# Attention and spectral mixing on one core: q and k transposed together, the opening sums in another order, idle products early

## The chip, the cores and the metric

The kernel runs on one core of a Trainium2 chip. The metric is the device time of one execution in microseconds (us). The time before is the median of three runs. The profile is one further execution, recorded by the hardware profiler.

The engines are called as in the profile: PE is TensorE's matrix product, PEld its weight load, DVE is VectorE, ACT is ScalarE, POOL is GpSimd and SP is SyncE. In this kernel POOL issues the loads from memory, SP issues the stores and the small copies.

## The reference

There are 8 batches and 8 heads, 576 tokens, 64 channels a head. The first part is causal attention with a bias that grows with the distance, the second part a mixing over the first 64 frequencies of the token axis, with a complex 512 x 512 weight for each frequency.

```python
scores = scale * np.matmul(q, k.transpose(0, 1, 3, 2))
cum = np.cumsum(np.maximum(s, 0.0), axis=-1)
bias = -(cum[:, :, :, None] - cum[:, :, None, :])
scores = np.where(causal, -1e9, scores + np.minimum(bias, 0.0))
attn = softmax(scores)
x = np.matmul(attn, v)                         # heads side by side: (8, 576, 512)

X = np.fft.rfft(x, axis=1)                     # Xr, Xi: its first 64 modes
Yr = einsum('bmd,mde->bme', Xr, w_r) - einsum('bmd,mde->bme', Xi, w_i)
Yi = einsum('bmd,mde->bme', Xr, w_i) + einsum('bmd,mde->bme', Xi, w_r)
u = x + np.fft.irfft(Yr + 1j * Yi, n=576, axis=1)
out = u + np.maximum(u @ w_ch, 0.0)
```

The two mode weights, `w_r` and `w_i`, are 64 x 512 x 512 numbers each.

## The kernel before, in words

**Order.** The order of the work on every engine is the order in which the program writes it. Nothing is moved by a planner. Each engine works through its own list, and an instruction that must wait holds back all that follows it on the same engine.

**Attention.** A step `n` (0 to 31) is one batch and one pair of heads: `g = n // 8` is the group of 128 channels, `b = n % 8` the batch. The loop at L564 writes for each step, in this order: the loads for step `n + 3` and some blocks of mode weights; `scores(n, 0)`; `av(n - 1, 1)`; the products of the mode blocks that are due; `transposes(n + 1, 0)`; `scores(n, 1)`; in the last six steps `first_transposed`; `transposes(n + 1, 1)`; `fft(n - 1)`; `av(n, 0)`; and in the last six steps `first_product`, `first_transposed`, `first_product`.

**The transposes.** q and k of a step lie together in one tile `qk2`: partitions 0 to 63 hold q of two heads, 64 to 127 hold k, and each partition holds a run of 18 tokens of one head. `transposes(n, half)` (L332) turns 9 of the 18 tokens of each run. For each it makes one product for q and one for k, 64 x 64 each (L340), into the partition halves of one tile `tr_ps`; that tile has one buffer (L557). Then two copies of 576 elements a partition (L344) take the result to `qt` and `kt`. For half 0 both are on DVE; for half 1 q is on DVE and k on ACT.

**Mode weights.** They come in 128 blocks of 512 KB, four for each of the 8 chunks `c` of 8 modes and each of the 4 groups `g`, two transfers a block. All are issued by POOL (L234), in order, between the loads of q, k and v, into a ring of tiles. `modes(g, c)` (L455) makes 16 products from the four blocks of a chunk: `x` = 0 and 1 use `w_r`, `x` = 2 and 3 use `w_i`. Results of the groups 0 to 2 are added up in `y_acc`; group 3 follows after attention.

**After attention.** The loop at L833 goes over the chunks 0 to 5 of group 3. After a chunk's products DVE makes `yb`, PE transposes it (`y_transposed`), ACT copies it out, and from chunk 4 on PE multiplies it by `w_ch` (`y_times_wch`). `work()` fills in between with products of x and `w_ch` for output pairs that end later. `gather` reorders the rows of several chunks for the inverse transform. A pair is two tiles of 128 tokens; pairs 0 and 1 are finished first. For each, `x_transposed(i)` (L629) transposes x by 8 or 16 products and two DVE copies, and `x_times_wch(i, False)` (L644) makes 8 products of 512 columns. Pair 0's stand in chunk 5, pair 1's stand in chunk 6, at L853 and L855, between the products of chunk 6 and its `y_times_wch`.

**Chunk 7.** L868 calls `modes` with work in between: before `x` = 2 it does `first_u` (pair 0's sum u: x, the rows of chunks 0 to 5, chunk 6) and `first_z(0)`, before `x` = 3 it does `first_z(1)`. `first_z` needs `vb6`, which is chunk 6's product with `w_ch`; `first_u` doesn't. After `x` = 3 come chunk 7's own `yb`, its transpose, its product, and then a written list of steps (L924) that finishes the 18 pairs.

Of the kernel before, what the change touches and what calls it, by code (L numbers as in the profile page):

```python
# [9 lines left out]
FP32 = mybir.dt.float32  # L10
FP16 = mybir.dt.float16
BF16 = mybir.dt.bfloat16
# [6 lines left out]
def kernel(  # L19
# [11 lines left out]
    nc = tc.nc  # L31
    B, H, S, D = q.shape
    NM = moe_w_r.shape[0]
    DM = H * D
    P = 128
# [4 lines left out]
    NG = DM // P  # L40
# [6 lines left out]
    NCK = NM // MC  # L47
# [4 lines left out]
    RP = P // 4  # L52
    R = S // RP
    RH = R // 2
    W = 2 * P
    NWN = S // W
    NK = 2 * NWN
    HM = NM // 2
    HP = P // 2
# [3 lines left out]
    negm_np = np.concatenate(  # L63
        [np.where(2 * np.arange(P)[:, None] + r > np.arange(W)[None, :], -1.0e9, 0.0) for r in range(2)],
        axis=1,
# [55 lines left out]
    NQ = 2  # L121
    qt = [ap_.tile([P, 2, S], BF16, name=f"qt{i}") for i in range(NQ)]
    kt = [ap_.tile([P, 2, S], BF16, name=f"kt{i}") for i in range(NQ)]
# [3 lines left out]

    v2 = [ap_.tile([P, 2 * NWN * W + P], FP16, name=f"v2_{i}") for i in range(NV)]

# [3 lines left out]
    for w in range(NWN):  # L133
        for r in range(2):
            poff.append(poff[-1] + SP - w * W)
    p_sb = [ap_.tile([P, poff[-1]], FP16, name=f"p_sb{i}") for i in range(NP_)]
    p4 = [ap_.tile([P, P], FP16, name=f"p4_{i}") for i in range(2)]

    temp = xs_flat[1].bitcast(FP32)
    ident32, negm32, s_sb = temp[:, :P], temp[:, P : P + 2 * W + NL], temp[:NPAIR, -S:]  # L140
    ident16 = ap_.tile([P, P], BF16, name="ident16")
# [4 lines left out]
    loaded = {}  # L146
# [98 lines left out]
    for n in range(N):  # L245
# [3 lines left out]
        while nt < min(w, len(wq)):  # L249
            i = ring_of(nt)  # L250
# [36 lines left out]
    with tc.tile_pool(name="cum_psum", bufs=1, space=PSUM) as cpsum:  # L287
        spos = s_sb
        zer, cum = (p_sb[i][:NPAIR, :].bitcast(FP32)[:, :S] for i in (0, 1))
        nc.vector.memset(zer, 0.0)  # L290
        nc.vector.tensor_scalar(out=spos, in0=s_sb, scalar1=0.0, scalar2=None, op0=ALU.max)
        nc.vector.tensor_tensor_scan(
            out=cum, data0=spos, data1=zer, initial=0.0, op0=ALU.add, op1=ALU.add
        )
        nc.vector.tensor_scalar(out=ncum_sb, in0=cum, scalar1=-8.0, scalar2=None, op0=ALU.mult)
        ct_ps = cpsum.tile([P, NK + 1, NPAIR], FP32, name="ct_ps")
        keys = cum[:, : NF * P].rearrange("c (w p r) -> c w r p", p=P, r=2)
        for x in range(NK):
            nc.tensor.transpose(
                ct_ps[:, x, :], keys[:, x // 2, x % 2, :], ident32[:NPAIR, :NPAIR]  # L300
            )

        tl = p_sb[2][:NPAIR, :].bitcast(FP32)[:, : 2 * NL].rearrange("p (x t) -> p x t", x=2)
        for x in range(2):
            nc.vector.tensor_copy(out=tl[:, x, :], in_=cum[:, (NT - 1) * P :])
        nc.tensor.transpose(
            ct_ps[:, NK, :], tl.rearrange("p x t -> p (x t)"), ident32[:NPAIR, :NPAIR]
        )
        nc.vector.tensor_copy(out=cumt_sb, in_=ct_ps)
        for x in range(2):  # L310
            rows = slice(NL * x, NL * x + NL)
            nc.vector.tensor_copy(
                out=cumt4[rows, :], in_=cumt_sb[rows, NK, x::2]
            )
# [17 lines left out]
    def transposes(n, half):  # L332
        if n >= N:
            return
        src = loaded[n][:, n % 2, :].rearrange("p (r d) -> p r d", d=D)[:, half * RH : half * RH + RH]
        ps = trpool.tile([P, RH, 2 * RP], BF16, name="tr_ps", tag="tr")
        for r in range(RH):
            for i in range(2):
                rows = slice(HP * i, HP * i + HP)
                nc.tensor.transpose(ps[rows, r, :], src[rows, r, :], ident16[rows, rows])  # L340
        for i, dst in enumerate((qt, kt)):
            copy = (nc.vector.tensor_copy, nc.scalar.copy)[half * i]
            to = dst[n % NQ][:D].rearrange("d h (p r) -> d h p r", r=R)
            copy(  # L344
                out=to[:, :, :, half * RH : half * RH + RH],
                in_=ps[HP * i : HP * i + HP].rearrange("d r (h p) -> d h p r", h=2),
            )

    def scores4(n, ps):

# [205 lines left out]
    with tc.tile_pool(name="sc_psum", bufs=2, space=PSUM) as scpool, \  # L556
# [7 lines left out]
        for n in range(N):  # L564
# [11 lines left out]
            i = first_pairs[n - N + len(first_pairs)] if n >= N - len(first_pairs) else None  # L576
# [52 lines left out]
    def x_transposed(i):  # L629
        xts[i] = xt_sb[len(xts) % 2]  # L630
        for x, (b, T) in enumerate(pairs[i]):
            ps = upool.tile([P, DT, P], FP32, name="xt_ps", tag="u")
            for rows, bb, ident in parts(b, T):
                for dt in range(DT):
                    nc.tensor.matmul(
                        ps[:, dt, rows], x_all[: rows.stop - rows.start, dt, bb, T, :],
                        ident, start=True, stop=True, skip_group_check=True,
                    )
            nc.vector.tensor_copy(out=xts[i][:, x], in_=ps)  # L639

    def start_z(i, x):
        zs[i, x] = zpool.tile([P, DM], FP32, name="z_ps", tag=f"z{i % 2}{x}")

    def x_times_wch(i, last):  # L644
        for x in range(2):
            start_z(i, x)
            for dt in range(DT):
                nc.tensor.matmul(  # L648
                    zs[i, x], xts[i][:, x, dt, :], wch_sb[:, dt, :],
                    start=(dt == 0), stop=(last and dt == DT - 1), skip_group_check=True,  # L650
                )
# [25 lines left out]
    def y_times_wch(c, yt):  # L677
        vp = auxpool.tile([P, DM], FP32, name="v_ps", tag="aux")
        for dt in range(DT):
            nc.tensor.matmul(  # L680
                vp, yt[:, dt, :], wch_sb[:, dt, :], start=(dt == 0), stop=(dt == DT - 1)
            )
        vb = spool.tile([P, DM], FP16, name="v_sb", tag="v")
        nc.vector.tensor_copy(out=vb, in_=vp)
        spread(c, 1, vb)
        return vb

    def gather(c0, c1, turns, kinds):

        n = 2 * MC * (c1 - c0)  # L690
        rows = slice(2 * MC * c0, 2 * MC * c1)
        ng = P // n
        for b0 in range(0, B, ng):
            for which in kinds:
                ps = auxpool.tile([P, DM], FP32, name="g_ps", tag="aux")
                for dt in range(DT):
                    for g in range(ng):
                        op = yt_first[:, dt, : c1 - c0].rearrange("p c (x b) -> p (c x) b", b=B)
                        nc.tensor.matmul(
                            ps[n * g : n * g + n, :] if which else ps[n * g : n * g + n, bass.ts(dt, P)],  # L700
                            op[:, :, b0 + g],
                            wch_sb[:, dt, :] if which else ident16h,
                            start=(dt == 0 or not which), stop=(dt == DT - 1 or not which),
                            tile_position=(0, n * g), skip_group_check=True,
                        )
                for g in range(ng):
                    dst, src = yv[rows, b0 + g, which, :], ps[n * g : n * g + n, :]
                    if g % 2:
                        nc.vector.tensor_copy(out=dst, in_=src)
                    else:  # L710
                        nc.scalar.copy(out=dst, in_=src)
            if b0 // ng in turns:
                work()
# [119 lines left out]
    for c in range(NCK - 2):  # L833
        yb = modes(NG - 1, c)
        for x in range(TAKE[c] - 1):
            work()
        if c == NCK - 3:
            x_transposed(0)
        yt = y_transposed(yb, c)
        if TAKE[c]:  # L840
            work()
        if c >= NY:
            if c == NCK - 3:
                x_times_wch(0, False)
            y_times_wch(c, yt)
            if c == NCK - 3:
                gather(NY, NCK - 2, (), (0,))
        elif c == NY - 1:
            gather(0, NY, (1, 3), (1, 0))
    assert not order_z and not ahead  # L850
    c = NCK - 2
    yb6 = modes(NG - 1, c)
    x_transposed(1)  # L853
    yt = y_transposed(yb6)
    x_times_wch(1, False)  # L855
    vb6 = y_times_wch(c, yt)


    def first_u():
        add_x(0)  # L860
        add_y(u_of(0), 0, 0, slice(0, GK))
        add_last(u_of(0), 0, yb6, c=0)

    def first_z(i):
        add_y(z_of(i), i, 1, slice(0, GK))
        add_last(z_of(i), i, vb6, c=0)

    yb = modes(NG - 1, NCK - 1, {2: lambda: (first_u(), first_z(0)), 3: lambda: first_z(1)})  # L868

    yt = spool.tile([P, DT, P], FP16, name="yt_sb", tag="yt")  # L870
    for x in range(2):
        dts = slice(x * DT // 2, (x + 1) * DT // 2)
        ps = auxpool.tile([P, DT // 2, P], FP16, name="yt_ps", tag="aux")
# [49 lines left out]
    for step in (  # L923
# [8 lines left out]
        i = int(step[1:].rstrip("ab"))  # L932
# [34 lines left out]
```

The softmax here doesn't subtract the row's maximum and nothing guards it: scores larger than these inputs give would overflow.

## Time and profile before

| | |
|---|---|
| time before, median of three runs | 443.91 us (443.87 to 444.06) |
| span of the profiled execution | 442.4 us |
| mean granted TensorE clock | 0.916 |
| PE busy | 340.4 us, 77% |
| DVE busy | 253.3 us, 57% |
| ACT busy | 226.2 us, 51% |
| POOL busy, most of it issuing loads | 246.1 us, 56% |
| moved by DMA | 93.25 MB, mean 211 GB/s |

A busy share is an average over stages with different limits. The stages are: attention to 336 us, the chunks 0 to 6 of group 3 from 336 to 403 us, chunk 7 to 411 us, and the finishing of the pairs to the end. The chain of waits follows the work back from the last instruction, each time to what released it. A granted clock of 0.50 means that products take twice as long as at 1.00.

### The profile page before, as it was taken

The page shows a single profiled execution, that of the slowest core. Times are in us where ns is not written, and L with a number is a line of the kernel's source. Part 1 is how long each engine was busy: PE and PEld are TensorE (multiplying, and loading weights), DVE is VectorE, ACT ScalarE, POOL GpSimd, SP SyncE. Part 2 cuts the span into 40 slices and gives each one's busy share as a digit, 9 for nine tenths or more (in the row PEclk, how much of TensorE's full clock was granted, in tenths as well). Part 3 has the DMA queues.
Part 4 walks back from the last instruction along what each step waited for, and adds up shares of the span by engine and source line. Part 5 has one row for each costly group of instructions (what it writes and reads, how often), then busy time and mean ns, then how long its engine had stood idle before and what let it go on. Part 6 is the DMA issues. An engine that isn't in the chain of part 4 may idle for free.

```text
span 442.4 us, 10783 instructions
## 1 busy us (share of the span) xinstructions
PE 340.4 (77%) x4364; PEld 208.2 (47%) x4411; DVE 253.3 (57%) x574; ACT 226.2 (51%) x421; POOL 246.1 (56%) x385
## 2 busy tenths in 40 slices
PE   1788988988776996593946918888887987759994
PEld 0455665655444653361634505555653445423441
DVE  7766776665645664462633605767655454442696
ACT  1476787365645643472543604665660534320794
POOL 7766565565565656455655546455544444440495
PEclk9998999998969798987895978999997999988998
DMA  9999999999999999999999999999999999997498
GB/s 180 202 208 204 204 206 205 206 207 206 208 195 206 205 208 205 209 206 209 203 206 206 208 207 198 207 206 206 202 209 211 209 209 210 210 217 150 147 388 344
DMA packets 72768, 93.25 MB, mean 211 GB/s; under 512 B 29760, under 2 KB 31296, under 8 KB 72720
## 3 DMA queue, kind: packets, MB, share of 16 engines
q0 software_dynamic: 63408, 81.29, 104.9%
q1 hardware_dynamic: 9312, 11.29, 7.6%
q8 instruction: 34, 0.56, 0.5%
q14 instruction: 14, 0.11, 0.1%
HBM read 163.51 MB, written 9.44 MB: 391 GB/s over the span
## 4 chain that ended last, share of the span: by engine, by line
DMA 60%; PE 19%; DVE 7%; POOL 6%; issue 4%; ACT 2%; POOLq 0%; DVEq 0%
DMA w_sb<-in_moe_w_i_dram 31%; DMA w_sb<-in_moe_w_r_dram 16%; DMA qk<-in_k_dram 8%; PE yp L463 4%; PE sc_ps L382 3%; DMA x_all<-in_moe_w_r_dram 2%; POOL w_sb L234 2%; DMA qk<-in_q_dram 2%; PE sc_ps L376 2%; DMA y_acc<-in_moe_w_r_dram 2%; PE z_ps L546 2%; DVE xt L538 2%; DVE xs L453 1%; PE z_ps L648 1%; PE av_ps L418 1%
## 5 line engine op out<-in xcount | busy, mean ns | idle before, releaser
L390 ACT ACTIVATE p_sb<-sc_ps,cumt_sb 128x576 f16<-128x576 f32 (+1 forms) x256 | 141.7, 635 | 34.3 <-PE sc_ps L382 33.9
L234 POOL DMA_DIRECT2D w_sb<-in_moe_w_r_dram x120 | 71.2, 595 | 63.2 <-DMA w_sb<-in_moe_w_i_dram 16.7
L234 POOL DMA_DIRECT2D w_sb<-in_moe_w_i_dram x120 | 70.9, 593 | 53.0 <-DMA w_sb<-in_moe_w_i_dram 18.7
L344 DVE COPY qt<-tr_ps 64x576 bf16<-64x576 bf16 x64 | 47.8, 747 | 55.7 <-PE tr_ps L340 55.6
L234 POOL DMA_DIRECT2D v<-in_v_dram x72 | 52.0, 722 | 36.6 <-DMA w_sb<-in_moe_w_r_dram 7.6
L382 PE MATMUL sc_ps<-qt,kt 128*128 128x320 bf16 (+2 forms) x337 | 66.7, 303 | 7.2 <-ACT kt L344 3.4
L340 PE MATMUL tr_ps<-ident,qk 64*64 64x64 bf16 x1152 | 35.4, 206 | 38.9 <-DMA qk<-in_k_dram 18.0
L463 PE MATMUL yp<-w_sb,xs 128*32 128x512 bf16 (+1 forms) x480 | 43.2, 413 | 23.8 <-DMA w_sb<-in_moe_w_i_dram 16.8
L361 ACT ACTIVATE p<-sc_ps,cumt 128x64 f16<-128x64 f32 x32 | 10.0, 313 | 88.7 <-PE sc_ps L357 88.7
L376 PE MATMUL sc_ps<-negm,ident 128*128 128x256 bf16 x256 | 53.8, 295 | 0.0
L382 PEld LDWEIGHTS <-kt 128*128 128x128 bf16 x384 | 39.0, 105 | 31.1 <-ACT kt L344 8.8
L340 PEld LDWEIGHTS <-qk 64*64 64x64 bf16 x1152 | 26.9, 119 | 55.2 <-DMA qk<-in_k_dram 19.0
L418 PE MATMUL av_ps<-v,p_sb 128*128 128x65 f16 x1024 | 43.8, 197 | 1.4 <-DVE x_all L428 1.0
L418 PEld LDWEIGHTS <-p_sb 128*128 128x128 f16 x1024 | 37.4, 99 | 8.5 <-DVE x_all L428 3.7
L453 DVE CAST xs<-ft_ps 64x128 bf16<-64x128 f32 x128 | 36.6, 286 | 3.7 <-PE ft_ps L443 2.2
L463 PEld LDWEIGHTS <-xs 128*32 128x32 bf16 (+1 forms) x512 | 19.3, 144 | 41.3 <-DMA w_sb<-in_moe_w_i_dram 15.0
L423 DVE TENSOR_REDUCE den<-av_ps 128x5 f32<-128x10 f32 x64 | 10.8, 169 | 41.4 <-PE av_ps L418 40.4
L428 DVE TENSOR_TENSOR x_all<-av_ps,rcp 128x320 f16<-128x320 f32 x64 | 31.5, 492 | 2.2
L344 ACT COPY kt<-tr_ps 64x576 bf16<-64x576 bf16 x32 | 22.9, 715 | 15.4 <-DVE qt L344 14.8
L443 PE MATMUL ft_ps<-Ff_sb,x_all 128*64 128x192 f16 (+1 forms) x320 | 25.2, 274 | 1.0 <-DVE x_all L428 1.0
L648 PE MATMUL z_ps<-wch_sb,xs 128*128 128x512 f16 x96 | 25.3, 412 | 0.2 <-DVE xs L639 0.2
L344 DVE COPY kt<-tr_ps 64x576 bf16<-64x576 bf16 x32 | 24.4, 762 | 0.4
(113 smaller groups left out, 423.9 us busy)
## 6 DMA issues: line engine op xcount, KB each, us to landing
w_sb<-in_moe_w_r_dram POOLq DMA_DIRECT2D x120, 256.0 KB, 8.4
w_sb<-in_moe_w_i_dram POOLq DMA_DIRECT2D x117, 256.0 KB, 9.0
out_dram<-r_w SPq DMA_DIRECT2D x16, 512.0 KB, 2.8
v<-in_v_dram POOLq DMA_DIRECT2D x72, 64.0 KB, 7.4
qk<-in_q_dram POOLq DMA_DIRECT2D x15, 288.0 KB, 8.3
qk<-in_k_dram POOLq DMA_DIRECT2D x15, 288.0 KB, 9.2
x_all<-in_moe_w_i_dram POOLq DMA_DIRECT2D x6, 256.0 KB, 8.0
y_acc<-in_moe_w_r_dram POOLq DMA_DIRECT2D x4, 256.0 KB, 7.0
```

What stands on the lines that cost most here:

```text
L234: nc.gpsimd.dma_start(out=dst, in_=src)
L340: nc.tensor.transpose(ps[rows, r, :], src[rows, r, :], ident16[rows, rows])
L344: copy(out=to[:, :, :, half * RH : half * RH + RH], in_=ps[HP * i : HP * i + HP].rearrange("d r (h p) -> d h p r", h=2),)
L376: nc.tensor.matmul(ps[:, bass.ds(w * S, W)], ident16, negm[:, bass.ts(r, W)], start=True, stop=False, skip_group_check=True,)
L382: nc.tensor.matmul(ps[:, c0 : c0 + i1 - i0], keys[:, w, r, :], qh[:, i0:i1], start=False, stop=True, skip_group_check=True,)
L390: nc.scalar.activation(out=pt[:, poff[x] : poff[x] + S - w * W], in_=ps[:, w * S : (w + 1) * S - w * W], func=ACTF.Exp, bias=cumt_sb[:, x, ...
L418: nc.tensor.matmul(ps[:, I, r : r + NCH], lhsT, rhs, start=(i == 0), stop=(i == len(todo) - 1), skip_group_check=True,)
L428: nc.vector.tensor_tensor(out=x_all[:, g, b, :, D * h : D * h + D], in0=ps[:, :, 1 : NCH], in1=rcp.unsqueeze(2).to_broadcast([P, NT, D]), ...
L443: nc.tensor.matmul(ps[HP * q_ : HP * q_ + HP].rearrange("p h f -> p (h f)"), x_all[:nT, g, b, T, q_::2], Ff_sb[:nT, T, :], start=(T == 0), ...
L453: nc.vector.tensor_copy(out=xs[g % 2][HP * h : HP * h + HP, q_, :, h, :, b, :], in_=a)
L463: nc.tensor.matmul(ps[32 * cg : 32 * cg + 32, :], cols[k0:, q_, 1 - ri, :, c * MC // 2 + cg], wt[(g, c, ri, cg // 2)][k0:, 2 * (cg % 2) + ...
L648: nc.tensor.matmul(zs[i, x], xts[i][:, x, dt, :], wch_sb[:, dt, :], start=(dt == 0), stop=(last and dt == DT - 1), skip_group_check=True,)
```

## The change

It has three parts.

1. **q and k transposed together.** A product now takes 64 channels of all 128 partitions, q and k at once: its result has 64 partitions, with 64 columns of q and 64 of k side by side. Tokens 0 to 8 of each run go to the first half of the result's partitions (`y` = 0), tokens 9 to 17 to the second (`y` = 1). Half 0 does token indices 0 to 4 of both, 10 products; half 1 indices 5 to 8, 8 products. The copies are now by token half and by q or k: four of 320 elements for half 0, four of 256 for half 1. The aim is fewer products.
2. **Idle products early.** 50 products of the identity with 64 of its own columns, whose result nobody reads, stand on PE ahead of the first transposes of the cumulative sums. The aim is a TensorE that has left its slow clock when attention starts.
3. **Opening sums re-ordered.** Pair 1's `x_transposed` and `x_times_wch` go from chunk 6 into chunk 5; and in chunk 7 both `first_z` stand before `x` = 2, `first_u` before `x` = 3. The aim is less work on PE behind the last weights.

```diff
+    SPLIT = (0, (RH + 1) // 2, RH)
...
+        idle_ps = cpsum.tile([P, HP], FP32, name="idle_ps")
+        for i in range(50):
+            nc.tensor.matmul(idle_ps, ident16, ident16[:, :HP], start=True, stop=True, skip_group_check=True)
...
-        src = loaded[n][:, n % 2, :].rearrange("p (r d) -> p r d", d=D)[:, half * RH : half * RH + RH]
-        ps = trpool.tile([P, RH, 2 * RP], BF16, name="tr_ps", tag="tr")
-        for r in range(RH):
-            for i in range(2):
-                rows = slice(HP * i, HP * i + HP)
-                nc.tensor.transpose(ps[rows, r, :], src[rows, r, :], ident16[rows, rows])
-        for i, dst in enumerate((qt, kt)):
-            copy = (nc.vector.tensor_copy, nc.scalar.copy)[half * i]
-            to = dst[n % NQ][:D].rearrange("d h (p r) -> d h p r", r=R)
-            copy(
-                out=to[:, :, :, half * RH : half * RH + RH],
-                in_=ps[HP * i : HP * i + HP].rearrange("d r (h p) -> d h p r", h=2),
-            )
+        r0, r1 = SPLIT[half : half + 2]
+        src = loaded[n][:, n % 2, :].rearrange("p (y r d) -> p y r d", y=2, d=D)
+        ps = trpool.tile([P, SPLIT[1], P], BF16, name="tr_ps", tag="tr")
+        for r in range(r0, r1):
+            for y in range(2):
+                nc.tensor.transpose(ps[HP * y : HP * y + HP, r - r0, :], src[:, y, r, :], ident16)
+        for y in range(2):
+            for i, dst in enumerate((qt, kt)):
+                copy = nc.scalar.copy if half and i else nc.vector.tensor_copy
+                to = dst[n % NQ][:D].rearrange("d h (p y r) -> d h p y r", r=RH, y=2)
+                copy(
+                    out=to[:, :, :, y, r0:r1],
+                    in_=ps[HP * y : HP * y + HP, : r1 - r0, HP * i : HP * i + HP].rearrange(
+                        "d r (h p) -> d h p r", h=2
+                    ),
+                )
...
             if c == NCK - 3:
                 x_times_wch(0, False)
+                x_transposed(1)
             y_times_wch(c, yt)
             if c == NCK - 3:
                 gather(NY, NCK - 2, (), (0,))
+                x_times_wch(1, False)
...
-    x_transposed(1)
     yt = y_transposed(yb6)
-    x_times_wch(1, False)
     vb6 = y_times_wch(c, yt)
...
-    yb = modes(NG - 1, NCK - 1, {2: lambda: (first_u(), first_z(0)), 3: lambda: first_z(1)})
+    yb = modes(NG - 1, NCK - 1, {2: lambda: (first_z(0), first_z(1)), 3: first_u})
```

## The prediction

> **What bounds the kernel now.** I read the strip of 40 slices first, then the queues, then the chain in order of time, and last the single transfers and windows around 400 us.
>
> ```profile
> DMA  9999999999999999999999999999999999997498
> q0 software_dynamic: 63408, 81.29, 104.9%
> ```
>
> For 36 of 40 slices, to 398 us, the DMA engines are over 90% busy, and the queue of loads that POOL fills asks for more than the whole span of 16 engines. So attention and the chunks 0 to 6 run beside a stream of loads that has no gap to give. Windows of 2 us between 20 and 396 us hold 184 to 225 GB/s, nearly all 195 to 213. The chain in order of time says what happens when the stream nears its end:
>
> ```profile
> 386.01 10.89 DMA w_sb<-in_moe_w_i_dram
> 396.91 0.04 issue
> 396.95 1.07 PE yp L463 x4
> 398.02 0.96 PE xt_ps L635 x16
> 398.98 0.54 PE yt_ps L672 x4
> 399.52 3.18 PE z_ps L648 x8
> 402.70 0.86 PE v_ps L680 x4
> 403.56 0.59 PE yp L463 x8
> ...
> 406.43 0.58 PE yp L463 x4
> ...
> 408.00 0.60 PE yp L463 x4
> ```
>
> From 396.95 to 408.6 PE is never idle, so 4.14 us of pair 1's work (0.96 + 3.18) look like a straight saving. They aren't, because eight more transfers were issued after the one that landed at 396.9. The last of them in the timeline, and the answer for its tile:
>
> ```profile
> 397.19 0.59 POOL L234 DMA_DIRECT2D w_sb<-in_moe_w_i_dram  x1 [0.70 <-DMA w_sb<-in_moe_w_i_dram]
> ```
> ```profile
> DMA to landing us min/median/max: 10.2/10.2/10.2
> ```
>
> It lands at 397.19 + 10.2 = 407.4. The same reading of the other seven gives 398.2, 399.5, 400.8, 402.0 for chunk 7's `w_r` and 403.3, 405.4, 406.2 for the first three of its `w_i`. The four products of `x` = 3 need the last one, and they start at 408.0. PE is thus only 0.6 us behind the stream. That 0.6 us is what part 3 can earn while the stream stays where it is.
>
> The windows of the clock:
>
> ```profile
> 392.30:395.70 3.40, 1.09 (x10) 0.48 (x10) 2.08 (x4) 1.73 (x3) 1.42 (x3) 0.96 1.10 208
> 395.70:399.10 3.40, 2.15 (x24) 1.26 (x25) 1.05 (x3) 0.00 (x0) 1.18 (x2) 0.50 1.13 220
> 399.10:402.50 3.40, 3.40 (x12) 1.29 (x11) 0.85 (x2) 0.58 (x1) 0.00 (x0) 0.54 1.12 210
> ```
>
> PE was busy a third of the first window and then ran at half clock (third number from the right) to 402.3. That is why eight products of 512 columns took 3.18 us there, against 1.90 us for the same eight at 387.8.
>
> **What the Trainium skill says.** "TensorE: Matmul & The Clock Gate", Part 1: the clock is halved after an idle window of about 3.4 us and restored after a busy one, and the windows run freely. The trace agrees: restored at 344.2 and 402.3, which is 17 times 3.41 us apart; half busy (336 us) was not enough to keep it, a full window restored it. "PSUM — Partial Sum Buffer", Terms: two engines on one bank and quadrant at once collide, so their accesses must be kept apart. In this trace they are kept apart by tile, even where the partitions differ: ACT's first k copy waited for DVE's q copy of the other half, though its input was long ready.
>
> ```profile
> 14.05 0.75 DVE L344 COPY qt<-tr_ps 64x576 bf16<-64x576 bf16 x1 [0.79 <-PE tr_ps L340]
> ```
> ```profile
> 14.83 0.71 ACT L344 COPY kt<-tr_ps 64x576 bf16<-64x576 bf16 x1 [12.58 <-DVE qt L344]
> ```
>
> "DMA: Bandwidth & Descriptors", Queues, rings and completion order: an engine takes turns between queues. So a small copy from SP takes its share at once and delays the weights; no run yet shows how much.
>
> **Part 1, the transposes.** A step had 36 products; now 18. Before, 18 took 0.47 us; with 0.206 for one, that is (0.47 - 0.206) / 17 = 16 ns each. The new ones have twice the columns. Products into two partition halves do run side by side here (four of L755, 512 columns, took 0.43 us, two at full width also 0.43), so a pair of 128 columns costs about a quarter of 214 ns: 10 products 5 x 53 + 206 = 0.47 us, 8 products 0.42. PE gains nothing to speak of; without the overlap it would lose 0.4 us a step.
>
> The copies cost more. DVE's 128x256 and 128x512 copies from `v_ps` take 424 and 692 ns: 156 + 1.047 ns an element, which gives 759 for 576 where the rows show 747 to 762. So 320 elements take 491 and 256 take 424 ns. Half 0: 4 x 491 = 1.96 us for 0.747 + 0.762 = 1.51, plus 0.45. Half 1 on DVE: 0.85 for 0.75, plus 0.10. ACT: its 256- and 512-element copies take 372 and 589, so two of 256 take 0.75 to 0.9 for 0.715. DVE in all: 32 x 0.55 = 18 us more.
>
> There is a new wait. The four copies of half 1 read one tile in the order DVE, ACT, DVE, ACT, so DVE's second must wait for ACT's first, and that stands behind the four exponentials of `scores(n, 1)`. In the step at 285 us these end at 289.03 and DVE would be at its second copy at 289.0; it gets it at 289.55 instead. Behind it on DVE wait the four `xs` casts, the division of `av` and the cast `xt` (done at 291.53), for which PE waited 0.99 us before `first_product`. I get 0.45 + 0.10 + 0.55, about 1.1 to 1.2 us a step on that path; 0.55 if the copies of different halves need not wait, 1.7 if ACT's copies are slower.
>
> In the steps up to 25 PE waits for q and k (30 us in all) and for weights (17 us), which hides it. In the last six, from 276 us, PE waits for no load; five of them have transposes, so attention ends some 6 us later (3 to 8.5). Who notices? Weight block k of the last groups takes the tile of block k - 11. I put the issue times beside the products' times: the tightest are block 107, issued 5.6 us after its tile came free, and block 123, 3.2 us. A later issue must moreover first eat the 10 us of transfers that are queued. PE itself has waits of 1.9 us at 355.7 and about 0.7 at 385 to give back, and 2 us at 395. So some 3 us may be left at chunk 5; the stream does not stop.
>
> **Part 2, the idle products.** At half clock a column takes 427 / 512 = 0.83 ns, so 50 of 64 columns take 2.7 us. Their input is there at 6.57, and the next PE work waited to 9.73 for the scan on DVE. Hidden; if each also paid for its own weight load, 107 ns, they would end at 11.9 and attention would start 2 us later, into waits for q and k. Cost at the end: 0 both ways.
>
> **Part 3.** Pair 1's two parts go into chunk 5. `x_transposed(1)` takes 0.64 us there (as at 360.7) and two DVE copies of 0.65 ahead of `v_sb`; the gather and chunk 6's `yp` tile move by 0.7. `x_times_wch(1)` takes 1.9 and fills PE's wait of 1.88 us for DVE before 393.7. Chunk 6 then still waits for 396.9. From there: 0.65 products, 0.75 `y_sb`, 0.4 to 0.6 transpose, 0.65 ACT, 0.9 to 1.75 `v_ps`, 0.75 `v_sb`: `vb6` at 401.2 to 402.2. `x` = 1 waits for 402.0. Both `first_z`, 0.86 + 0.98 warm, to 404.2, or 3.5 cold, to 405.9. `x` = 2 waits for 405.4. `first_u` is six products of 0.214, 1.3 us. PE is at `x` = 3 at 407.1 warm, about 407.5 if the clock comes back at 405.7 (two windows after 398.9). So the stream decides: 407.4. But `v_sb`'s 128 KB, sent at 404.3 before, now go out at 402, in full traffic. The hardware queue's 7.6% of 442.4 us for 11.29 MB is 3.0 us a MB, so up to 0.4 us. I take 0.25: `x` = 3 at 407.7 instead of 408.0. What follows is unchanged. Sum: 443.9 - 0.3 = 443.6.
>
> **The rivals.**
> A, the saving comes through: the stream itself gets earlier, or the tail loses more than its last wait. For: PE is gapless to 408.6. Against: the landing at 407.4. The full 4.1 us would give 439.8; a stream 0.5 us earlier and the 0.6 give 442.8, the likely form.
> B, the clock: PE is idle more between 397 and 405, stays at half clock to as late as 408.8, and `first_u` takes 2.6. Then `x` = 3 starts at 408.9: 444.9. For: 1.1 us busy of the 3.4 before 399. Against: both `first_z` keep PE busy from 402.4.
> C, attention's copies: the lag is 8 us or more, chunk 6 starts at 400 or later and blocks come late: x = 3 at 409.5, 445.4. For: DVE is the chain in the last steps. Against: the tiles' slack.
>
> **How the numbers follow.** Stream decides, 443.6: 0.62. A 0.17, B 0.12, C 0.09. The range takes in A's likely form and B and the near side of C: 442.7 to 445.2. Faster by 0.2% is below 443.0: A, 0.18. Slower is above 444.8: B and C, 0.20. Within: 0.62.
>
> **What would show it.** The last weight lands at 407.2 to 407.9 and `x` = 3 follows within 0.2 us. `tr_ps` copies: 490 and 424 ns, DVE some 18 us busier, a wait of DVE for ACT `kt`. Attention ends at 339 to 345 instead of 336. The DMA strip stays at 9 to slice 36. I am wrong if the last landing moves by over 1 us, or if `x` = 3 starts well after it.

## The result and the profile after

The changed kernel takes 450.51 us (median of six runs, 448.81 to 451.57). The kernel before takes 444.17 us beside it (443.87 to 445.12). The ratio is 1.0136, 95% interval 1.0112 to 1.0159: slower by 6.3 us. The prediction was 443.6 us with a range from 442.7 to 445.2.

In the changed kernel's line numbers everything below the transposes stands 7 lines lower than before: the products `yp` are L470 instead of L463, the loads are L235 instead of L234. These are lines of the profile page after: busy time, the strip of 40 slices, the queue of loads, the shares of the chain by engine, and two groups of copies (busy us, mean ns, then the idle time before them and its releaser).

```profile
PE 339.7 (76%) x3847; PEld 200.9 (45%) x3885; DVE 274.2 (61%) x670; ACT 232.5 (52%) x453; POOL 246.3 (55%) x385
DMA  9999999999999999999999999999999999994398
q0 software_dynamic: 63408, 81.29, 103.7%
PE 33%; DVE 27%; DMA 24%; ACT 9%; issue 4%; POOL 2%; SPq 0%; POOLq 0%; DVEq 0%; ACTq 0%
L349 DVE COPY qt<-tr_ps 64x256 bf16<-64x256 bf16 (+1 forms) x128 | 65.3, 510 | 50.6 <-PE tr_ps L344 29.0
L349 ACT COPY kt<-tr_ps 64x256 bf16<-64x256 bf16 x64 | 30.4, 475 | 31.4 <-DVE qt L349 29.9
```

PE has not gained (340.4 us before). DVE is busy 20.9 us more, ACT 6.3 us more. The strip still reads 9 to slice 36, so by the strip alone nothing has changed. The chain has: before, DMA held 60% of it, PE 19% and DVE 7%. Now PE and DVE hold 60% together, and the loads 24%.

The chain in order of time, near the end of the loads (start, us, what):

```profile
387.96 1.83 PE z_ps L655 x8
389.79 1.07 PE yp L470 x14
390.89 0.70 DVE y_sb L494
...
393.81 1.05 PE yp L470 x11
394.88 0.57 DVE y_sb L494
...
404.83 0.70 DVE y_sb L494
406.01 0.59 ACT yt_sb L681
406.65 1.04 PE v_ps L687 x4
407.69 0.99 PE yp L470 x8
...
413.82 0.60 PE yp L470 x4
```

Before, this chain ran through the landing of a weight block at 396.9. Here no load stands in it from 380 us on. The four products of `x` = 3 start at 413.8 instead of 408.0, and the 5.8 us between are nearly the whole loss: the program ends 33.9 us after the last `y_sb` addition (DVE's first work on chunk 7's products) starts in this kernel, 33.7 us in the one before.

PE's waits between 336 and 412 us say the same (us in total, times, longest). Before, one line of its answer was

```profile
PE yp L463 <- DMA w_sb<-in_moe_w_i_dram: 4.2, 3, 2.1
```

After, the answer has no line with a load in it. It begins

```profile
PE yt_ps L679 <- DVE y_sb L494: 3.6, 4, 1.7
PE g_ps L706 <- DVE yv L716: 2.0, 2, 1.0
PE ft_ps L450 <- DVE x_all L435: 1.0, 1, 1.0
```

The last weight block lands at 408.6 us, 1.2 us later than before, and `x` = 3 starts some 5 us behind it; before, it was 0.6 us. Both are signs that the prediction had named for being wrong. So the end is no longer set by the loads but by the work after attention, and that starts later. The last two divisions of the attention on DVE, before and then after:

```profile
330.99 0.49 DVE L428 TENSOR_TENSOR x_all<-av_ps,rcp 128x320 f16<-128x320 f32 x1
334.26 0.49 DVE L428 TENSOR_TENSOR x_all<-av_ps,rcp 128x320 f16<-128x320 f32 x1
```
```profile
342.12 0.49 DVE L435 TENSOR_TENSOR x_all<-av_ps,rcp 128x320 f16<-128x320 f32 x1
345.39 0.49 DVE L435 TENSOR_TENSOR x_all<-av_ps,rcp 128x320 f16<-128x320 f32 x1
```

The last one is 11.1 us late. I call this the lag. Of it 5.3 us are absorbed (I call this the slack) and 5.8 us remain. The stretch from this division to the last `y_sb` shows where the 5.3 us come from. Before, PE is busy 60.4 of its 74.4 us; after, 58.7 of 69.0 us. So 3.7 us are idle time of PE that is gone, the waits for weights above all. The other 1.6 us are busy time: PE runs at half clock for 10.2 us of the stretch after and for 13.7 us before, one window of the clock less.

One step's copies in the timeline of the kernel after (DVE and ACT only; in brackets the idle time before and its releaser):

```profile
276.39 0.50 DVE L349 COPY qt<-tr_ps 64x320 bf16<-64x320 bf16 x1
276.80 0.49 DVE L349 COPY kt<-tr_ps 64x320 bf16<-64x320 bf16 x1
277.31 0.55 DVE L349 COPY qt<-tr_ps 64x320 bf16<-64x320 bf16 x1
277.75 0.52 DVE L349 COPY kt<-tr_ps 64x320 bf16<-64x320 bf16 x1
...
278.91 0.57 DVE L349 COPY qt<-tr_ps 64x256 bf16<-64x256 bf16 x1
279.52 0.57 ACT L349 COPY kt<-tr_ps 64x256 bf16<-64x256 bf16 x1
280.13 0.43 DVE L349 COPY qt<-tr_ps 64x256 bf16<-64x256 bf16 x1 [0.64 <-ACT kt L349]
...
280.58 0.37 ACT L349 COPY kt<-tr_ps 64x256 bf16<-64x256 bf16 x1 [0.49 <-DVE qt L349]
```

The 0.64 us ahead of DVE's last copy is the new wait that the prediction had named. DVE has it in each of the five steps with transposes after 276 us, 3.2 us together.

The lag does not grow evenly, though. These are the starts of `x_all` of head 0 by step, late against before, in us (worked out from the timelines):

```text
step                        26    27    28    29    30    31
after                      1.1   2.5   5.4   8.1   9.4  11.1
```

Two steps cost 1.3 to 1.4 us. Three cost 1.7 to 2.9. What differs there is in the windows of the clock (PE busy us first, granted clock third from the right):

```profile
287.94:291.36 3.42, 2.83 (x46) 1.88 (x44) 2.70 (x7) 2.69 (x6) 2.39 (x5) 1.00 1.21 203
291.36:294.77 3.41, 1.39 (x10) 0.54 (x9) 2.55 (x8) 0.91 (x2) 2.08 (x4) 1.00 1.24 206
294.77:298.18 3.41, 3.19 (x27) 2.21 (x26) 0.00 (x0) 2.44 (x5) 1.87 (x4) 0.55 1.15 209
```

PE stood behind the delayed `xs` and `xt` of DVE (0.87 and 1.15 us), was busy 1.39 of 3.41 us, and then ran at half clock for a window. It happened three times, at 295.1, 308.8 and 332.7 us. These times are 4 and 7 times 3.41 us apart, so the windows go on in even steps; in the three windows just ahead of them PE was busy 41% each time. No sharp bound shows: in the same trace windows of 56% and 59% (from 281.5 and 319.0 us) kept the clock and one of 71% (from 346.3 us) lost it. Before, the clock stood at 1.00 from 270 to 336 us.

### The profile page after: what moved, and what is told of

It reads as the page before. It is cut to its first block, busy times and chain, and to the rows that moved or that the text cites. A ratio compares the mean times of both kernels' runs of the same rounds, so it can differ in the third digit from the quotient of the medians.

```text
span 448.4 us, 9886 instructions
## 1 busy us (share of the span) xinstructions
PE 339.7 (76%) x3847; PEld 200.9 (45%) x3885; DVE 274.2 (61%) x670; ACT 232.5 (52%) x453; POOL 246.3 (55%) x385
## 4 chain that ended last, share of the span: by engine, by line
PE 33%; DVE 27%; DMA 24%; ACT 9%; issue 4%; POOL 2%; SPq 0%; POOLq 0%; DVEq 0%; ACTq 0%
DMA w_sb<-in_moe_w_i_dram 11%; DMA w_sb<-in_moe_w_r_dram 9%; DVE qt L349 7%; PE yp L470 7%; DVE xs L460 5%; PE z_ps L655 5%; PE av_ps L425 4%; ACT p_sb L397 4%; DVE x_all L435 3%; DVE kt L349 3%; PE sc_ps L389 3%; ACT kt L349 3%; PE tr_ps L344 2%; DMA qk<-in_k_dram 2%; PE sc_ps L383 2%
## 5 line engine op out<-in xcount | busy, mean ns | idle before, releaser
L235 POOL DMA_DIRECT2D w_sb<-in_moe_w_i_dram x120 | 71.3, 599 | 62.6 <-PE yp L470 29.2
L235 POOL DMA_DIRECT2D w_sb<-in_moe_w_r_dram x120 | 71.4, 601 | 51.3 <-DMA w_sb<-in_moe_w_i_dram 16.0
L349 DVE COPY qt<-tr_ps 64x256 bf16<-64x256 bf16 (+1 forms) x128 | 65.3, 510 | 50.6 <-PE tr_ps L344 29.0
L389 PE MATMUL sc_ps<-qt,kt 128*128 128x320 bf16 (+2 forms) x346 | 68.7, 305 | 18.0 <-ACT kt L349 13.4
L235 POOL DMA_DIRECT2D v<-in_v_dram x72 | 52.1, 723 | 39.1 <-DMA w_sb<-in_moe_w_i_dram 8.5
L344 PE MATMUL tr_ps<-ident,qk 128*64 128x128 bf16 x576 | 30.1, 235 | 33.4 <-DVE kt L349 21.6
L383 PE MATMUL sc_ps<-negm,ident 128*128 128x256 bf16 x256 | 54.7, 299 | 0.0
L470 PE MATMUL yp<-w_sb,xs 128*32 128x512 bf16 (+1 forms) x480 | 43.3, 439 | 8.7 <-DMA w_sb<-in_moe_w_i_dram 4.9
L349 ACT COPY kt<-tr_ps 64x256 bf16<-64x256 bf16 x64 | 30.4, 475 | 31.4 <-DVE qt L349 29.9
L344 PEld LDWEIGHTS <-qk 128*64 128x64 bf16 x576 | 19.2, 115 | 47.9 <-DVE kt L349 27.7
L349 DVE COPY kt<-tr_ps 64x320 bf16<-64x320 bf16 x64 | 32.5, 508 | 0.0
L470 PEld LDWEIGHTS <-xs 128*32 128x32 bf16 (+1 forms) x512 | 18.7, 146 | 28.9 <-issue 14.9
L450 PE MATMUL ft_ps<-Ff_sb,x_all 128*64 128x192 f16 (+1 forms) x320 | 23.0, 256 | 1.0 <-DVE x_all L435 1.0
```

Of the source, the lines that this page charges most:

```text
L235: nc.gpsimd.dma_start(out=dst, in_=src)
L344: nc.tensor.transpose(ps[HP * y : HP * y + HP, r - r0, :], src[:, y, r, :], ident16)
L349: copy(out=to[:, :, :, y, r0:r1], in_=ps[HP * y : HP * y + HP, : r1 - r0, HP * i : HP * i + HP].rearrange("d r (h p) -> d h p r", h=2),)
L383: nc.tensor.matmul(ps[:, bass.ds(w * S, W)], ident16, negm[:, bass.ts(r, W)], start=True, stop=False, skip_group_check=True,)
L389: nc.tensor.matmul(ps[:, c0 : c0 + i1 - i0], keys[:, w, r, :], qh[:, i0:i1], start=False, stop=True, skip_group_check=True,)
L450: nc.tensor.matmul(ps[HP * q_ : HP * q_ + HP].rearrange("p h f -> p (h f)"), x_all[:nT, g, b, T, q_::2], Ff_sb[:nT, T, :], start=(T == 0), ...
```

## The experiments

Theory at the start: the copies and their waits hold the attention back, and the work after it is late by the lag less the slack of some 5 us. Rivals: part 2 or part 3 is to blame; the two-sided form of the products is; the loads stop, because POOL must wait for tiles of the ring. The times of before beside each run are medians of 24 to 35 runs: 444.46 us for the first four, 444.12 for the next four, 444.38 for the last four.

**1. Part 1 alone.** The kernel before with the change's new `SPLIT` and `transposes`.

```diff
+    SPLIT = (0, (RH + 1) // 2, RH)
...
+        r0, r1 = SPLIT[half : half + 2]
+        src = loaded[n][:, n % 2, :].rearrange("p (y r d) -> p y r d", y=2, d=D)
+        ps = trpool.tile([P, SPLIT[1], P], BF16, name="tr_ps", tag="tr")
...
```

> The kernel before with part 1 alone (transposes of q and k together, eight smaller copies). Theory L (the copies lengthen attention's last steps on DVE, PE falls some 11 us behind, weight tiles come free late, and the chunks that follow are bound by PE and no longer by the loads): attention's last x_all at 343 to 347 us, POOL idle for PE yp by 5 to 6 us at a time after 320 us, and at least the whole loss, 450 to 452 us, perhaps more since pair 1's work then stands behind the last weights again. Theory O (pair 1's work in chunk 5 is what costs): 443.5 to 445 us, attention at most 2 us late at the end.

Measured 453.41 us, ratio 1.0202 (1.0177 to 1.0227). This is 1.4 us above the theory's range, for which it had left room. The lag is 13.0 us. Part 1 alone costs more than the whole change.

**2. Parts 2 and 3.** The kernel after with before's `transposes`.

```diff
-    SPLIT = (0, (RH + 1) // 2, RH)
...
+        ps = trpool.tile([P, RH, 2 * RP], BF16, name="tr_ps", tag="tr")
...
+        for i, dst in enumerate((qt, kt)):
+            copy = (nc.vector.tensor_copy, nc.scalar.copy)[half * i]
```

> The changed kernel with the transposes and copies of before (parts 2 and 3 alone). Theory L: the loads stay the bound, attention ends at 334 us as before, 443.3 to 444.3 us. Theory O: 446 to 450 us with chunk 6's products later than 398 us although attention ends on time. Theory C (clock alone: PE idle behind chunk 6 stays at half clock): attention on time, chunk 7's x = 3 at 408.5 or later, 444.5 to 445.5 us.

Measured 445.86 us, ratio 1.0027 (1.0017 to 1.0037), in none of the three ranges. The attention is in time, and the last `y_sb` starts at 408.58 us as before. Still 1.4 us are lost, and they appear behind the last operation of DVE, which ends at the same time as before. Experiments 5 and 9 explain it.

**3. The order of the copies.** The kernel after, and in a half first both q copies, then both k copies. DVE's two then come first, and it never waits for ACT.

```diff
-        for y in range(2):
-            for i, dst in enumerate((qt, kt)):
+        for i, dst in enumerate((qt, kt)):
+            for y in range(2):
```

> The changed kernel with the four copies of a half in the order q, q, k, k, so that DVE's second copy of half 1 no longer stands behind ACT's first. Theory L with the wait as its larger part: some 0.65 us less a step on DVE, attention ends 3 to 5 us earlier than in the changed kernel, and 445.5 to 448 us. Theory L with the added copy time and the clock as the larger part: less than 1.5 us gained, 449 to 450.5 us. Theory O: no difference from the changed kernel.

Measured 445.36 us (442.84 to 449.00 in twenty runs, a wide spread), ratio 1.0018 (1.0001 to 1.0035), 0.1 us below the range. The lag is 6.4 us, and the last `y_sb` starts at 408.92. The same step in its timeline:

```profile
276.50 1.06 DVE L349 COPY qt<-tr_ps 64x320 bf16<-64x320 bf16 x2
277.57 1.07 DVE L349 COPY kt<-tr_ps 64x320 bf16<-64x320 bf16 x2
...
279.28 1.00 DVE L349 COPY qt<-tr_ps 64x256 bf16<-64x256 bf16 x2
280.31 1.19 DVE L460 CAST xs<-ft_ps 64x128 bf16<-64x128 f32 x4
...
280.37 0.96 ACT L349 COPY kt<-tr_ps 64x256 bf16<-64x256 bf16 x2 [0.76 <-PE av_ps L425]
```

The copies are the same and take as long, but no bracket stands at DVE. An order of two loops is worth 5 of the 6 us. Part of this comes by the clock: during attention PE was at half clock for one window here (from 305.3 us), in the change for three.

**4. Before's products, copies cut in two.** The kernel before, its 64 x 64 products kept, each copy of 9 tokens cut into 5 and 4, in the order q, k, q, k.

```diff
+        for a0, a1 in ((0, (RH + 1) // 2), ((RH + 1) // 2, RH)):
...
+                    in_=ps[HP * i : HP * i + HP, a0:a1].rearrange("d r (h p) -> d h p r", h=2),
```

> The kernel before, its own transposes and order, with each copy out of the transposes cut into one of five and one of four tokens (320 and 256 elements), in the order q, k, q, k. If the copies and their waits are the cause: attention ends 5 us or more late and 448 to 452 us. If it is the form of the products (128 rows, 128 columns, two halves of the result): as before, 443.5 to 445 us.

Measured 449.88 us, ratio 1.0113 (1.0085 to 1.0141), lag 11.4 us. The form of the products is out. More and smaller copies in this order do it with before's products.

**5. Part 2 alone.** The kernel before with the 50 idle products.

```diff
+        idle_ps = cpsum.tile([P, HP], FP32, name="idle_ps")
+        for i in range(50):
+            nc.tensor.matmul(idle_ps, ident16, ident16[:, :HP], start=True, stop=True, skip_group_check=True)
```

> The kernel before with part 2 alone, the 50 idle products at the start. The run of parts 2 and 3 together was 1.4 us above before (445.86 against 444.46); this run and the next split that. Theory: the products lie in TensorE's opening wait (50 x 53 ns = 2.6 us, from 6.6 to 9.2 us) and nothing after them moves, so the time is 444.2 to 444.8. Rival: they cost it all, 445.6 to 446.1.

Measured 445.72 us, ratio 1.0035 (1.0022 to 1.0047): the time that the rival gave. The products do lie in PE's opening wait (6.62 to 9.47 us), the first product after them starts at 9.74 as before, and the last `y_sb` at 408.41. The loss is in the stores of the result. The answer for the tensor `out_dram` of this kernel ends with

```profile
DMA to landing us min/median/max: 2.0/4.0/4.5
```

and that of the kernel before with

```profile
DMA to landing us min/median/max: 2.0/2.8/3.1
```

The median of the same stores is 1.2 us later, while PE, DVE and ACT are busy as long as before from the last `y_sb` on (27.3, 24.6 and 24.3 us in both). What else is on the DMA engines then? The queue of instructions. The kernel before has, in the list of queues,

```profile
q8 instruction: 34, 0.56, 0.5%
```

34 packets of 16 KB. In the trace PE has 4364 products and 4411 weight loads, 8775 instructions; 0.56 MB over these is 64 bytes each, so the packets are PE's, 256 instructions in each. 50 idle products are 100 instructions, and every later packet comes 100 instructions earlier in the program. In the kernel before the last one comes at 411.3 us, ahead of the big stores; here it comes at 426.4 us. The stores issued up to 423.7 us land in 2.0 to 3.1 us, as before. The one issued at 425.0 us takes 4.5 us, and all that follow take 3.6 to 4.2.

**6. Part 3 alone.** The kernel before with the re-ordered opening sums.

```diff
+                x_transposed(1)
...
+                x_times_wch(1, False)
...
-    yb = modes(NG - 1, NCK - 1, {2: lambda: (first_u(), first_z(0)), 3: lambda: first_z(1)})
+    yb = modes(NG - 1, NCK - 1, {2: lambda: (first_z(0), first_z(1)), 3: first_u})
```

> The kernel before with part 3 alone, the re-ordered opening sums. Theory: part 3 brings nothing while the stream of loads is the bound, and costs what the small spreading copies and the last landing do to each other: x=3 of the last block starts within 0.3 us of before's 408.0 and the time is 444.6 to 446.0. Rival: part 3 gains what the prediction gave it, 444.0 or below.

Measured 444.50 us, ratio 1.0004 (0.9996 to 1.0013): no difference from before, and 0.1 us below the range. In the profiled execution PE ran at half clock from 399.4 to 406.3 us and reached `x` = 3 at 409.0, not within 0.3 us of 408.0; the last weights landed at 408.6 there. In the profile of experiment 2, with the same order, they landed at 407.8 and `x` = 3 started at 407.89.

**7. Part 1 alone, copies in the order q, q, k, k.** The diffs of experiments 1 and 3 together.

> The kernel before with part 1 alone, and within a half the copies in the order q, q, k, k. Theory: VectorE's wait behind ScalarE's copy is what drives the loss of part 1 (453.41 with the order q, k, q, k). Without it the attention's last x_all starts 6 to 7 us late instead of 12.9, the slack of some 5 us between the attention and the last landing takes nearly all of it, and the time is 444.8 to 446.5. Rival: part 3 was what saved the same order in the run with all three parts (445.36); without it 447 to 449.

Measured 447.01 us, ratio 1.0048 (1.0031 to 1.0064). The lag is only 5.0 us, below the 6 to 7 that were expected, but the time is 0.5 us above its range. 0.9 us of the loss are slower stores (3.8 us). Of the rest, PE was at half clock for 20.5 us after attention, against 10.2 us in experiment 3. Whether part 3 spared the clock there or the windows fell better by chance is not separated.

**8. A clock kept up.** The kernel after, with idle products ahead of PE's two waits of the steps 26 to 30. They write to room added to `tr_ps`, which nobody reads.

```diff
...
                 first_product(i, 0)
+                warm(12 if n + 1 < N else 0)
                 first_transposed(i, 1)
+                warm(20 if n + 1 < N else 0)
```

> The changed kernel with 12 and 20 idle 64-column products before TensorE's two waits of the steps 26 to 30 (for xs, 0.87 us, and for xt, 1.15 us; some 0.6 and 1.1 us of products). Theory: half of the attention's lag of 11.1 us comes from three stretches at half clock between 294 and 336 us, which follow TensorE's sparse windows before them; with the products the clock stays at 1.00 from 276 to 336, the lag falls to 6 to 8 us and the time to 445.3 to 447.5. Rival: the lag is all copies and waits, and the half clock only falls where TensorE waits anyway: lag 10.5 to 12, time 450 to 451.5.

Measured 448.63 us, ratio 1.0089 (1.0072 to 1.0106). The windows from 276 to 336 us of the kernel after, and then of this one:

```profile
276.00:336.00 60.00, 46.18 (x523) 28.50 (x527) 37.21 (x93) 32.39 (x63) 31.04 (x51) 0.92 1.16 208
```
```profile
276.00:336.00 60.00, 51.78 (x746) 34.47 (x746) 39.52 (x99) 33.80 (x66) 32.53 (x54) 1.00 1.16 208
```

The clock stays at 1.00, and the lag falls to 8.2 us although it is already 2.4 us at step 25 (0.8 us in the kernel after). From step 25 on it grows by 5.8 us in place of 10.3. The half clock was worth 4.5 us of the lag. (In experiments 1 and 11, which also have three windows at half clock there, it grows by 10.4 and 10.7 us.) The time misses its range by 1.1 us: a packet of instructions fell among the stores, and from the last `y_sb` to the end it takes 35.7 us instead of 33.9.

**9. 128 idle products.** Experiment 5 with 128 for 50.

```diff
-        for i in range(50):
+        for i in range(128):
```

> Part 2 alone again, with 128 idle products in place of 50. With 50, one of the 16 KB packets that bring TensorE its instructions fell at 427.9 us, among the stores of the result, whose median landing went from 2.8 to 4.0 us; in the kernel before the last such packet is at 412.8, ahead of the stores. A product is two instructions and a packet holds 256 instructions of 64 bytes, so 128 products shift the packets by a whole one: they should fall where before's fall. Theory (the packet's place is the cost): last packet near 413, stores 2.7 to 3.1 us, time 443.9 to 444.8, although the products now last 6.9 us and hold the opening up. Rival (the products themselves cost): 446.5 or more.

Measured 444.68 us, ratio 1.0008 (0.9997 to 1.0019). More than twice the products cost less: the stores land in 2.8 us again.

**10. The attention held back by something else.** The kernel before, its copies untouched, with 51 idle products, of 32 columns, ahead of `av(n, 0)` in the steps 26 to 30. They write to room added to `tr_ps`, which nobody reads.

```diff
...
             fft(n - 1)
+            warm(51 if 26 <= n < N - 1 else 0)
             av(n, 0)
```

> The kernel before, its copies untouched, with 51 idle products (some 2.75 us) ahead of av(n, 0) in each of the steps 26 to 30: 255 products, 13.8 us in all, 510 instructions, so that the instruction packets keep their places. Theory: what sets the end is only how late the attention ends, by whatever cause, less a slack of some 4 to 5 us: lag of the last x_all 10 to 13 us, TensorE waits for no weights after it, time 449 to 452. Rival: the loss belongs to the copies or to the stream's order, and idle products on TensorE ahead of a loads-bound tail cost little: 444 to 446.

Measured 453.01 us, ratio 1.0198 (1.0172 to 1.0225), 1 us above the range since the lag is 13.9 us and not 13 at most. The last `y_sb` is 8.8 us late, so 5.1 us were absorbed, and PE waits for no weights after attention. Lag alone does it, whatever makes it.

**11. The change without part 2.**

```diff
-        for i in range(50):
-            nc.tensor.matmul(idle_ps, ident16, ident16[:, :HP], start=True, stop=True, skip_group_check=True)
```

> The changed kernel without part 2. Theory of the instruction packets: 100 instructions fewer move the last packet from 419.4 to some 430 us, among the stores, which land in some 4 us in place of 2.9; the time is 451.2 to 452.2, so that part 2 saves a microsecond here and costs 1.6 alone. Rival (part 2's cost is its own): 448.9 to 449.5.

Measured 452.98 us, ratio 1.0186 (1.0164 to 1.0208), so 2.5 us above the change and 0.8 us above the range. The stores are as expected, 4.0 us; the lag is 12.0 us, 0.9 more than with part 2, and the slack some 1 us less, with one window more at half clock after attention. Why the lag is longer isn't traced further. In this company part 2 saves time; alone it costs some.

**12. The change with both remedies.** The order of experiment 3, and 10 and 16 idle products in the places of experiment 8.

> The changed kernel with both remedies: copies in the order q, q, k, k, and 10 and 16 idle products in the steps 26 to 30 (260 instructions, so the packets keep their places). Theory: what is left of the lag is the copies' own work, the last x_all is 3 to 5.5 us late, inside the slack; stores 2.7 to 3.1 us; time 443.9 to 445. Rival: the lag keeps 6 us or more, since the clock was high in most steps with this order already, and the time is that of the order alone, 445.4, or more.

Measured 443.87 us, ratio 0.9990 (0.9978 to 1.0003): the time of the kernel before. The lag is 4.8 us, and it grows by 0.5 us in the first of these steps and by 0.8 to 1.0 in the other four. The slack takes it all, and the time is at the lower end of the range. `x` = 3 starts at 407.2 us, right behind the landing of the last weights: the loads set the end again.

This also splits what the order is worth. With the clock at 1.00 in the last steps, the lag grows from step 25 on by 5.8 us in the order q, k, q, k (8) and by 4.9 and 4.3 us in the order q, q, k, k (7 and 12). So DVE's wait for ACT is worth 0.9 to 1.5 us of lag by itself; the rest of what the order saves in 3, as an estimate from these profiles, is the clock that it spares.

All kernels in one list, from their traces: the lag at step 31; the start of the last `y_sb`; the last 16 KB packet of instructions, counted from that `y_sb`; the median landing of the stores; and the time from that `y_sb` to the end of the span. (The packet times in the expectations of 9 and 11 were counted back from the end of the span and are about 1.5 us too high; here they are by the trace's clock.)

```text
kernel                  lag   last y_sb   packet   stores   y_sb to end
before                  0.0    408.62      +2.7     2.8       33.7
after                  11.1    414.44      +3.6     2.9       33.9
1 part 1               13.0    418.62     +12.6     4.0       34.8
2 parts 2 and 3         0.2    408.58     +18.3     4.2       35.2
3 order                 6.4    408.92      +3.5     2.8       33.7
4 split copies         11.4    415.43      +2.6     3.0       33.9
5 part 2                0.5    408.41     +18.0     4.0       34.9
6 part 3                0.2    409.69      +2.6     2.8       33.7
7 part 1, order         5.0    411.67     +12.6     3.8       34.6
8 clock                 8.2    410.95     +23.2     3.2       35.7
9 part 2, 128           0.2    409.29      +2.5     2.8       33.7
10 delay               13.9    417.40      +2.6     2.8       33.8
11 without part 2      12.0    416.35     +12.5     4.0       34.8
12 order and clock      4.8    407.85      +2.6     2.8       33.7
```

The big stores start 10 us after the last `y_sb`. Where the last packet comes before that, at most 3.6 us after the `y_sb`, the tail takes 33.7 to 33.9 us, eight times of eight. Where it comes among the stores, it takes 34.6 to 35.7 us, six times of six. In each of the six, the first store that takes over 4 us is one that is under way when the packet comes; those that have landed by then take within 0.5 us of before's time. "Runtime: NRT & Kernel Launch", Instruction fetch mechanics, in the Trainium skill says that each engine refills its instructions in blocks of 16 KiB, 256 instructions, by its own DMA queue, and calls the cost "mostly hidden". The sizes agree with this trace. The cost is hidden from PE, which in experiment 5 is busy as long as before after the last `y_sb`; it is not hidden from the stores, which from 420 to 440 us already move 370 to 408 GB/s in the kernel before.

The list also gives the slack, lag less lateness of `y_sb`. It follows the time that PE spends at half clock between attention and `y_sb`, which comes in windows of 3.41 us. The kernel before has four. With three windows (10.2 us) it is 5.1 to 6.1 us: 5.3 in the change, 6.1, 5.9 and 5.1 in 3, 8 and 10 (the 5.6 of 12 isn't its measure, since the loads set the end there). With four it is 4.6 and 4.3 us in 4 and 11. With five and six it is 3.0 and 2.0 us in 1 and 7.

What of the rival that the loads stop? They do. POOL's waits between 330 and 410 us, and one of them in the timeline after:

```profile
POOL w_sb L235 <- PE yp L470: 25.6, 6, 6.2
```
```profile
390.68 1.18 POOL L235 DMA_DIRECT2D w_sb<-in_moe_w_i_dram  x2 [6.22 <-PE yp L470]
```

Before, that wait was 0.9 us in all. From one window of 4 us to the next the transfers fall from 205 to 172 GB/s at 392 us. But PE waits for none of the weights, and in 1, 4, 7, 8, 10 and 11 as in the change `x` = 3 starts 1.6 us or more after the last of them has landed. So this is a consequence: PE frees tiles late because it is late. Whether a ring with more tiles would leave the time as it is was not tried.

## Why the prediction was wrong

**The stream as the bound before, and part 3.** Right in kind: experiment 6 shows no difference. The 0.3 us it gave to part 3 were not seen.

**PE and the copies.** Right in kind and in the sum, not in its terms. PE's busy time fell by 0.7 us. The copies were put at 491 and 424 ns; on DVE those of 320 elements took 521 (q) and 508 (k), those of 256 took 500. DVE was put at 18 us more and has 20.9. The wait for ACT was foreseen, and 1.1 to 1.2 us a step with it. At full clock experiment 8 shows 1.2 to 1.4 us in four steps and 0.5 in the other, 5.8 us in all. But of the rate 0.55 us were put to the copies and 0.55 to the wait; experiments 7 and 12, without the wait, still gather 4.9 and 4.3 us in the five steps, 0.9 to 1.0 a step. The copies were put too low and the wait too high, and that they add up as foreseen is luck.

**The lag: the step that failed.** "Attention ends some 6 us later (3 to 8.5)": 11.1 us. Five steps at the foreseen rate would be 5.5 to 6 us, and experiment 8 shows 5.8. What is missing in that sum is the clock. DVE's delays gather PE's waits in one window of 3.41 us; PE falls to half clock in three of the steps; and that is 4.5 us more. The rest, 0.8 us, was there at step 25. The prediction quoted "TensorE: Matmul & The Clock Gate", Part 1, and used it for chunk 6 only, where a thin window stood in the profile already. It did not ask which windows the change would thin out. The page speaks of an idle window; this trace, at 291.4 us, shows that one in which PE is busy 41% is enough, and the measurement decides.

**The slack.** The prediction found 1.9, 0.7 and about 2 us of PE's waits to give back, 4.6 us in all. The runs show 4.3 to 6.1 us unless PE loses more windows to the half clock. The size was right, and with a lag of 11.1 us it would have given a loss of 6.5 us where 5.8 were measured. The terms were so only in part: 3.7 us of the change's 5.3 are waits given back, and 1.6 are a window that happened to stay at full clock, which no sum had foreseen. "The stream does not stop" was wrong, but follows from the lag. The free time of ring tiles, 5.6 and 3.2 us, was not what set the end.

**Part 2.** Hidden in the opening, as it said. "Cost at the end: 0 both ways" was wrong: 1.6 us alone (its profile shows 1.2 of it behind the last `y_sb`), by the place of an instruction packet, and a saving of 2.5 us within the change, 0.9 of it by the same. No view that it read could show this, save the list of queues.

**The rivals.** C is what happened: lag over 8 us, chunk 6 after 400 us. It had a chance of 0.09 and a time of 445.4 us, since it took a lag just over its threshold, and not the whole of one. The half clock of B appeared in the profile of experiment 6, with `x` = 3 at 409.0 us, against the 408.9 us worked out. That they agree is luck, for the last weights landed at 408.6 there, 1.2 us later than the sum for B had them.

## What to carry to other kernels

- When an edit adds a wait to an engine that feeds TensorE, lay its delay into the clock's windows of 3.41 us: here each window that fell to 41% busy was followed by one at half clock, and that nearly doubled the lag that attention gathered (10.3 us for 5.8). Sum the waits that TensorE could give back, and compare them with the lag: what exceeds them is the loss, up or down by the windows that change their clock.
- Where two engines copy from one tile, write all copies of the one that is on the path first. Here that order of two loops was worth 5 us, the clock that it spared included.
- In a kernel that ends with stores at full rate, a count of TensorE's instructions anywhere earlier can move the end by 1 to 2 us, because it moves an instruction packet into the stores. Compare variants by the time from the last computed tile to the end as well, before crediting an edit.

## What the runs showed of the hardware

Unexpected was the size of the last point: one packet of 16 KB among the stores, which run at 370 to 408 GB/s in the kernel before, makes the landings that follow later, and the stores don't catch up to the end. In five runs of six the median landing rises from 2.8 us to 3.8 to 4.2. In the sixth, experiment 8, the packet came last, 23 us after the `y_sb`: the nine stores from then on took 4.4 to 5.0 us, the eleven before it hold the median at 3.2, and the tail was the longest of all. Why it costs about 2 us there and about 1 us in the others is open. The end comes 0.9 to 2.0 us later in the six.
